# Four FNet and GEGLU layers on one core: when raw w_down, turned z and the next statistics are fetched, and how w_down pieces lie in memory

## The chip, the cores and the metric

The kernel runs on one core of one Trainium2 chip. The metric is the time of one execution in microseconds of the device (us), as the median of the runs shown. The profile is of one more execution, whose own time stands beside its span below. Names of engines: TensorE is PE (its weight loads are PEld), VectorE is DVE, ScalarE is ACT, GpSimd is POOL, SyncE is SP. SP computes nothing here: it issues loads. POOL issues nearly all stores and some loads.

## What is computed

x is 2048 tokens of 512 numbers in float32. Two kinds of layer take turns, four layers in all:

```python
def mix(x):                                   # layers 0 and 2
    z = layernorm(x)
    a, b = z @ dft_hid_re.T, z @ dft_hid_im.T          # 512 x 512 each
    return x + dft_seq_re @ a - dft_seq_im @ b         # 2048 x 2048 each
def geglu(x):                                 # layers 1 and 3
    z = layernorm(x)
    return x + (gelu(z @ w_gate) * (z @ w_up)) @ w_down   # 512 x 1792, 1792 x 512
x = geglu(mix(geglu(mix(x))))
```

Both geglu layers use the same weights.

## The kernel before, in words

**Products.** Each float32 operand is split into a high part and a low part (`split`, L148: ACT writes the high part at L150, DVE the low part at L152), and `mm3` (L205) makes one product of three matmuls (L207 to L209), each 128x128 weights against 128x512. Two-by-two blocks are multiplied with seven products for eight. The seven left operands of a block have names: A11, A12, S1, S2, S3, S4 and A22; the S are sums and differences of the four corners. They are made once, kept in DRAM as "pieces" and loaded again: `wblocks` (wb in the profile) for w_gate and w_up, `wdd` (wc in the profile) for w_down. `pieces` pairs the names: (A11, A12), (S2, S3), (S1, A22), (S4). A piece is 256 KB: 128 partitions with 256 numbers of the high part and 256 of the low part.

**geglu(w, layer)** works on one half of the tokens (w = 0 or 1), in two parts of 512.
- *Up*: the loop over n = 0 .. 13 (`up`). Even n is w_gate, odd n is w_up, for two blocks of 128 of the 1792 columns. Each n has seven products of 6 matmuls (`product`, `first`, `second`). From n = 1 on, one product of w_down of 6 matmuls is put beside it (`beside`). `finished` takes the gelu at even n (ACT, L1014) and multiplies at odd n (DVE, L1028).
- *Late*: what is left of w_down, the list `down_order(layer, w)[1]`, 36 products of 6 matmuls where all seven pairs are done this way (`SEVEN` is 7; it is 5 in the last geglu). `prepared` splits their right operands, `ended` adds and turns the results, `rows_done` stores them.

**What sets the order.** Each engine takes its instructions in a fixed order, which follows the order of the program closely; a wait of one holds those behind it on the same engine. Work that is not part of the product at hand is kept in lists:
- `queue`: `step()` is called once at each product of up and after each late product, and runs one entry; `None` is an empty turn.
- `slow`: each PACE-th (9th) step also runs one entry of `slow`. For w = 0 it holds the eight layer norms of w = 1 (`block_steps`, `norm`). For w = 1 of layer 1 it holds `terms_ahead`: for eight blocks of 128 rows of layer 2 a load of x (L235, from SP), four ACT instructions (L565 to L570) and two on POOL, which give mean and variance.
- `down_making`: for each of the seven pairs k of w_down the entries "load" (`weight_steps`, `load`: three DMAs from SP, L956 to L958, 512 KB from wdc), "sums" (four DVE instructions, L190 and L183) and four times "divide" (split a piece pair and store it from POOL, L312 and L977). They are taken four at a time at six places of layer 0 (`down_pieces`, `DOWN_RUNS`), which is pairs 0 to 3, and then two at a time at the top of each `up(n)` with n above 2 in layer 1, w = 0: pairs 4 to 6.
- The stream of pieces (`items`, `load_next` at L328, `take`): a piece of w_down may be requested from SP when it is at most `NEAR` products ahead of the one taken: 2 in up, 6 in late.

**Turned z.** `norm` turns z in blocks of 32 on DVE and stores it from POOL (L676, tile `t`). `fetch(c)` (L687) reads it back with eight DMAs of 64 KB, 128 rows of 512 B each; for w = 1 they are issued on SP, 32 in all. `first`, `second`, `fourth` and `divide` of `block_steps` make the right operands of w = 1 of it (B11, B21, T1 .. T4, B22). In w = 0 of layers 1 and 3, at n = 13, what is left in `slow` is run, and the four fetches go to the front of the queue (`ahead_of_all`), so they are run at the products of n = 13. The queue of late then begins with four empty turns, followed by the 18 entries that use the fetched blocks. After late product 12, eight loads of w_gate/w_up pieces (`ahead`, L1004) are woven into it.

**How a w_down piece lies.** `kept` stores the high parts of two names as one row of 2 KB per partition, and the low parts as the next 2 KB. `down_piece` then reads one name as two runs of 1 KB: its half of the high row and its half of the low row. S4 is alone and is one row of 2 KB.

Of the kernel before, what the change touches and what calls it, by code (L numbers as in the profile page):

```python
# [17 lines left out]
ND = D // P  # L18
# [15 lines left out]
PACE = 9  # L34
# [5 lines left out]
LEAD = 3  # L40
NK = NS // 2
SEED_AT = 3
DOWN_RUNS = ((0,0,0,0),(4,4,4,0),(4,4,4,0),2)


@with_exitstack
def fnet_geglu(ctx: ExitStack, tc: tile.TileContext, x_in, ws, wh, wgu, wdn, wdc, out):
# [32 lines left out]
    nc = tc.nc  # L80
# [56 lines left out]
    def f32(ap):  # L137
        return ap.bitcast(F32)
# [72 lines left out]
    half = slice(0, 256), slice(256, 512)  # L211
# [21 lines left out]
    def x_load(layer, i, engine=nc.sync):  # L233
        t = sb.get()
        engine.dma_start(t, rows(layer, i))  # L235
        return t
# [26 lines left out]
    def x_seeded(b, rows):  # L263

        banks = []
        for i in rows:
            t = xrows.pop((b, i))
            banks.append(ps8.get())
            seed(banks[-1], t)
            sb.put(t)  # L270
        return banks
# [24 lines left out]
    wdd = {k: dram.tile([P, 7 * 512], F32, name=f"wc{k}") for k in range(NF // 2)}  # L296
    pieces = (("A11", "A12"), ("S2", "S3"), ("S1", "A22"), ("S4",))

    def down_piece(k, name):

        i = next(i for i, names in enumerate(pieces) if name in names)
        if i == 3:
            return wdd[k][:, 3 * 1024:]
        h = half[pieces[i].index(name)]
        return wdd[k][:, i * 1024:(i + 1) * 1024].rearrange("p (h c) -> p h c", h=2)[:, :, h]

    def halves(t):
        return t[:, :512], t[:, 512:]

    def kept(place, parts):  # L310
        for t, a in zip(parts, halves(place)):
            nc.gpsimd.dma_start(a, f32(t))  # L312
# [6 lines left out]
    def load_next():  # L319
        n = stream["loaded"]  # L320
        dtype, addresses, _, _ = items[n]
        raws[n] = []
        for a in addresses:
            t = sb.get(dtype)
            to = t if dtype == F32 else f32(t)
            if len(a.shape) == 3:
                to = to.rearrange("p (h c) -> p h c", h=2)
            stream["last"] = nc.sync.dma_start(to, a)  # L328
            raws[n].append(t)
        stream["loaded"] += 1  # L330
# [101 lines left out]
    def plan(layer):  # L432

        fore, steps = FORE[layer], []
        steps += [(b, "A11") for b in range(fore)] + [(b, "A12") for b in range(fore)]
        for b in range(NB):
            if b >= fore:
                steps += [(b, "A11"), (b, "A12")]
            products = [(b, "S2"), (b, EARLY_HID), (b, "S4"), (b, MID_HID), (b, LATE_HID)]
            steps += products  # L440
        return steps
# [6 lines left out]
    NP = NF // 2  # L448
# [62 lines left out]
                items.extend((F32, (wdn[f],), plain, None) for f in range(2 * SEVEN[layer + 1, w], NF))  # L511


    queue, slow, steps_done, down_making = [], [], [0], []

    def step():
        if queue:
            run = queue.pop(0)
            if run is not None:
                run()  # L520
        steps_done[0] += 1
        if slow and steps_done[0] % PACE == 0:
            slow.pop(0)()


# [47 lines left out]
    def terms_ahead(layer, i, n):  # L573

        if i == 0:
            fresh["terms"] = x_load(layer, 0)
        x, junk = fresh.pop("terms"), sb.get()
        if i + 1 < n:
            fresh["terms"] = x_load(layer, i + 1)
        known[layer, i] = norm_terms(layer, i, x, junk)  # L580
        sb.put(x, junk)
# [156 lines left out]
    def mix(layer):  # L738
# [44 lines left out]
        def down_pieces(b, at):  # L783
            for _ in range(DOWN_RUNS[at][b]):
                if layer == 0 and down_making:
                    down_making.pop(0)()

        def six(ps, name, k, start, stop, done=None):
            w = take()
            for c in range(2):  # L790
                mm3(ps[c], z_chunk(name, k, c), w, start, stop)
            sb.put(*w)
            if done:
                sb.put(*(zparts.pop((done, k)) if done[0] == "T" else [zparts.pop((done, k))]))
            step()
# [8 lines left out]
        def a11(b):  # L804
            chain = [ps8.get() for _ in range(2)]
            for k in range(NK):
# [6 lines left out]
                else:  # L813
                    six(chain, "B11", k, k == 0, k == NK - 1, "11" if b == NB - 1 else None)
                if b == FORE[layer] - 1 and k == SEED_AT:
                    a12_seeded(0)
# [5 lines left out]
        def a12_seeded(b):  # L822

            side_banks[b] = [ps8.get() for _ in range(2)]
            for c in range(2):
                seed(side_banks[b][c], sums[b][c])
                if b:
                    put_away((layer, b, c), sums[b][c])
# [8 lines left out]
        def a12(b):  # L837
# [5 lines left out]
            for k in range(NK):  # L843
                six(side, "B21", k, False, k == NK - 1, "21" if b == NB - 1 else None)
                if k == SEED_AT:
                    if b + 1 < FORE[layer]:
# [13 lines left out]
        def s2(b):  # L860
# [12 lines left out]
            for i, k in skewed(3):  # L873
# [4 lines left out]
                else:  # L878
                    six(three, "T3", k, k == 0, k == NK - 1)
                if i == 0 and k == SEED_AT:  # L880
                    hid_banks[b] = x_seeded(b, range(2))
# [39 lines left out]
        for n, (b, what) in enumerate(plan(layer)):  # L921
            if n == len(plan(layer)) - 1:
                if layer:
                    weight_load(0)
                    weight_load(1)
                while queue:
                    step()
            in_order[0] = layer or (b, what) not in plan(layer)[:2 * FORE[layer]]
            if layer == 0 and (b, what) == (0, "S2"):
                for k in range(NP):  # L930
                    load, making = down_weight_steps(k)
                    down_making.extend([load] + making)
            if what in stages:
                stages[what](b)
            else:
                hid_groups(b, what)
# [5 lines left out]
    wblocks = {n: dram.tile([P, 7 * 512], F32, name=f"wb{n}") for n in range(NF)}  # L942
# [3 lines left out]
    def weight_steps(n, raw=wgu, place=wblocks):  # L946

        src, v = [], {}

        def load():  # L950
            src.extend(sb.get() for _ in range(4))
            for i, names in enumerate((*pieces[:3], ("S4", "A21"))):
                for name, h in zip(names, half):
                    v[name] = src[i][:, h]
            with tc.issue_after(stream["last"].ins):
                nc.sync.dma_start(src[0], raw[n, :, :512])  # L956
                nc.sync.dma_start(v["A22"], raw[n, :, 512:768])
                nc.sync.dma_start(v["A21"], raw[n, :, 768:])  # L958

        def sums():  # L960
            before, in_order[0] = in_order[0], True
            plus(v["S1"], v["A21"], v["A22"])
            minus(v["S2"], v["S1"], v["A11"])
            minus(v["S3"], v["A11"], v["A21"])
            minus(v["S4"], v["A12"], v["S2"])
            in_order[0] = before

        def divide(i):
            def run():
                before, in_order[0] = in_order[0], True  # L970
                to = place[n][:, i * 1024:min((i + 1) * 1024, 7 * 512)]
                if i < 3:
                    t = split_slot(src[i])
                    kept(to, t)
                else:
                    t = (split_side(v["S4"]),)
                    nc.gpsimd.dma_start(to, f32(t[0]))  # L977
                if place is wblocks:
                    piece_here(n, i, t)
                else:  # L980
                    sb.put(*t)
                sb.put(src[i])
                in_order[0] = before
            return run

        return load, [sums] + [divide(i) for i in range(len(pieces))]

    def down_weight_steps(k):
        return weight_steps(k, wdc, wdd)
# [17 lines left out]
    def weight_load(n):  # L1007
        for i in range(len(pieces)):
            piece_load(n, i)
# [7 lines left out]
    def geglu(w, layer):  # L1017

        gs, h, acc = {}, {}, {0: [], 1: []}
# [31 lines left out]
        making = {}  # L1051
# [35 lines left out]
        def up(n):  # L1087
# [4 lines left out]
            if n > 2:  # L1092
                for _ in range(DOWN_RUNS[3]):
                    if down_making:
# [220 lines left out]
        before_mix = w == 1 and layer < 3  # L1315
        plain_down = (layer, w) not in SEVEN
        if before_mix:
            slow.extend((lambda k=k: terms_ahead(layer + 1, k, NK)) for k in range(NK))
        if w == 0:
            norms, others = block_steps(layer, 1)  # L1320
            slow.extend(norms)
            ahead_of_all = others[:ND]
        if not plain_down and layer == 1 or layer == 3:
            sb.reclaim("x")
        first(0)
# [14 lines left out]
        elif pairs == NP:  # L1340
            load_turned(0)
        if w == 0:
            queue.extend(([None] * 4 if ahead_of_all else []) + others[len(ahead_of_all):])
        elif before_mix:
            queue.extend((lambda k=k: first_rows(layer + 1, k)) for k in range(NK))
        ahead = [(lambda n=n, i=i: piece_load(n, i)) for n in range(2) for i in range(len(pieces))]
# [154 lines left out]
```

## Time and profile before

| | us |
|---|---|
| median of 3 runs | 1626.48 |
| the runs | 1619.25, 1629.77, 1626.48 |
| the profiled execution: its own time | 1617.86 |
| its span (first to last instruction) | 1615.7 |
| layer 0 (mix) ends, layer 1 begins on PE, about | 404 |
| granted TensorE clock, mean | 0.998 |

| DMA | |
|---|---|
| moved in the span | 419.14 MB, 259 GB/s mean |
| packets under 2 KB | 106592 of 258840 |
| issued from SP (q1) | 336.16 MB |
| issued from POOL (q0) | 81.55 MB |

How to read it: the page gives the busy time of each engine as a share of the span, and for groups of instructions (line, engine, operation, tiles) their busy time, the mean of one in ns, and the idle time just before them with what ended it. The view of waits names, for an engine, who it waited for: total us, number of waits, longest. The view of stretches gives length, busy time and count of instructions, the granted clock (1.00 is full), the DMA engines' mean busy share (it can exceed 1 a little, since packets overlap) and GB/s. The timeline lists instructions with start, duration and, in brackets, the idle time before it. An "SPq" row is the issue of a DMA, not its transfer.

### The profile page before, as it was taken

The page shows a single profiled execution, that of the slowest core. Times are in us where ns is not written, and L with a number is a line of the kernel's source. Part 1 is how long each engine was busy: PE and PEld are TensorE (multiplying, and loading weights), DVE is VectorE, ACT ScalarE, POOL GpSimd, SP SyncE. Part 2 cuts the span into 40 slices and gives each one's busy share as a digit, 9 for nine tenths or more (in the row PEclk, how much of TensorE's full clock was granted, in tenths as well). Part 3 has the DMA queues.
Part 4 walks back from the last instruction along what each step waited for, and adds up shares of the span by engine and source line. Part 5 has one row for each costly group of instructions (what it writes and reads, how often), then busy time and mean ns, then how long its engine had stood idle before and what let it go on. Part 6 is the DMA issues. An engine that isn't in the chain of part 4 may idle for free. (4 is left out here: it accounts for less than half of the span.)

```text
span 1615.7 us, 22644 instructions
## 1 busy us (share of the span) xinstructions
PE 1598.9 (99%) x7008; PEld 1317.2 (82%) x7008; DVE 1133.3 (70%) x1958; ACT 885.4 (55%) x1711; POOL 260.9 (16%) x469
## 2 busy tenths in 40 slices
PE   9999999999999999999999999999999999999998
PEld 7888888888788878788788888888888888888887
DVE  8997778797689784445879967777764457743574
ACT  8955466664667552645648545565555455433460
POOL 4112121242456101100031000101400000000001
PEclk9999999999999999999999999999999999999999
DMA  9878887996988899954986866878989676895445
GB/s 359 292 266 305 284 312 263 339 327 214 335 307 320 271 309 304 248 168 138 319 285 201 269 238 224 283 246 283 267 282 301 191 222 189 309 302 175 125 150 156
DMA packets 258840, 419.14 MB, mean 259 GB/s; under 512 B 28512, under 2 KB 106592, under 8 KB 257696
## 3 DMA queue, kind: packets, MB, share of 16 engines
q1 hardware_dynamic: 234480, 336.16, 65.2%
q0 software_dynamic: 24240, 81.55, 14.2%
q8 instruction: 55, 0.90, 0.2%
q14 instruction: 65, 0.53, 0.1%
HBM read 341.31 MB, written 76.28 MB: 258 GB/s over the span
## 5 line engine op out<-in xcount | busy, mean ns | idle before, releaser
L208 PE MATMUL p<-s,s 128*128 128x512 f32 x2320 | 902.6, 390 | 0.0
L209 PE MATMUL p<-s,s 128*128 128x512 f32 x2320 | 895.8, 390 | 0.0
L207 PE MATMUL p<-s,s 128*128 128x512 f32 x2320 | 870.9, 391 | 10.7 <-DMA s<-wc 4.2
L150 ACT ACTIVATE s<-s 128x512 fp32r<-128x512 f32 (+1 forms) x809 | 454.9, 607 | 264.0 <-DVE s L183 72.9
L152 DVE TENSOR_TENSOR s<-s,s 128x512 fp32r<-128x512 f32 (+1 forms) x809 | 510.8, 669 | 121.0 <-ACT s L150 102.4
L207 PEld LDWEIGHTS p<-s,s 128*128 128x128 f32 x2320 | 436.2, 188 | 104.8 <-DMA s<-wc 5.5
L208 PEld LDWEIGHTS p<-s,s 128*128 128x128 f32 x2320 | 436.6, 188 | 91.0 <-DVE s L152 0.7
L209 PEld LDWEIGHTS p<-s,s 128*128 128x128 f32 x2320 | 436.5, 188 | 90.4
L187 DVE TENSOR_TENSOR s<-s,p 128x512 f32<-128x512 f32 x188 | 127.5, 685 | 175.6 <-PE p L209 146.5
L183 DVE TENSOR_TENSOR s<-s,s 128x512 f32<-128x512 f32 (+1 forms) x374 | 224.8, 619 | 7.9 <-PE p L208 3.7
L194 ACT ACTIVATE s<-p 128x512 f32<-128x512 f32 x232 | 134.0, 594 | 112.0 <-PE p L209 107.6
L1014 ACT ACTIVATE s<-s 128x512 f32<-128x512 f32 x84 | 52.7, 629 | 69.1 <-DVE s L187 66.9
L568 POOL TENSOR_SCALAR rstd<-rstd 128x1 f32<-128x1 f32 x40 | 22.3, 556 | 347.4 <-ACT s L567 331.9
L152 DVE TENSOR_TENSOR s<-xwide,s 128x512 fp32r<-128x512 f32 x71 | 48.3, 687 | 33.9 <-ACT s L150 33.6
L1028 DVE TENSOR_TENSOR s<-s,p 128x512 f32<-128x512 f32 x56 | 38.4, 686 | 31.5 <-PE p L209 28.2
L312 POOL DMA_DIRECT2D wb<-s x84 | 45.8, 548 | 90.1 <-ACT s L150 61.5
L190 DVE TENSOR_TENSOR s<-s,s 128x512 f32<-128x512 f32 (+1 forms) x68 | 41.1, 613 | 16.5 <-DMA s<-wdc 9.8
L150 ACT ACTIVATE s<-xwide 128x512 fp32r<-128x512 f32 x71 | 43.1, 621 | 17.2 <-DVE xwide L183 6.6
L591 ACT ACTIVATE s<-s,shift,rstd 128x512 f32<-128x512 f32 x56 | 45.0, 811 | 11.3 <-DMA s<-x 5.7
L201 ACT ACTIVATE p<-p 128x512 f32<-128x512 f32 x56 | 32.7, 585 | 27.9 <-PE p L209 27.7
L1014 ACT ACTIVATE s<-p 128x512 f32<-128x512 f32 x28 | 16.7, 598 | 52.8 <-PE p L209 49.1
L565 ACT ACTIVATE s<-s 128x512 f32<-128x512 f32 x33 | 20.7, 627 | 42.1 <-DMA s<-x 22.2
(100 smaller groups left out, 601.5 us busy)
## 6 DMA issues: line engine op xcount, KB each, us to landing
s<-ws SPq DMA_DIRECT2D x384, 256.0 KB, 4.9
s<-wb SPq DMA_DIRECT2D x294, 256.0 KB, 4.9
s<-wc SPq DMA_DIRECT2D x182, 256.0 KB, 4.7
s<-wh SPq DMA_DIRECT2D x116, 256.0 KB, 5.1
wb<-s POOLq DMA_DIRECT2D x98, 256.0 KB, 4.7
s<-x SPq DMA_DIRECT2D x59, 256.0 KB, 5.2
xwide<-ws SPq DMA_DIRECT2D x50, 256.0 KB, 4.8
wc<-s POOLq DMA_DIRECT2D x49, 256.0 KB, 6.0
```

The lines of the kernel that those rows point to most:

```text
L150: newest["ACT"] = nc.scalar.activation(hi, src, AF.Copy)
L152: newest["DVE"] = nc.vector.tensor_tensor(lo, src, f32(hi), op=ALU.subtract)
L183: nc.vector.tensor_tensor(out, a, b, op=ALU.subtract)
L187: bank_read["DVE"] = nc.vector.tensor_tensor(out, a, b, op=ALU.add)
L190: nc.vector.tensor_tensor(out, a, b, op=ALU.add)
L194: bank_read["ACT"] = nc.scalar.activation(v, src, AF.Copy)
L207: nc.tensor.matmul(ps, ah, bh, start=start, stop=False, skip_group_check=True)
L208: nc.tensor.matmul(ps, ah, bl, start=False, stop=False, skip_group_check=True)
L209: nc.tensor.matmul(ps, al, bh, start=False, stop=stop, skip_group_check=True)
L312: nc.gpsimd.dma_start(a, f32(t))
L591: nc.scalar.activation(z, x, AF.Identity, bias=shift, scale=rstd)
L1014: nc.scalar.activation(t, g, AF.Gelu_apprx_tanh)
```

## The change

Four edits go together.

1. In `mix`, the list `down_making` is built with the load of a pair moved: pairs 0 to 3 keep "load k, sums k, four divides"; at pair 4 it is "load 4, load 5, sums 4, four divides", at pair 5 "load 6, sums 5, four divides", at pair 6 "sums 6, four divides".
2. `slow` of layer 1, w = 1 begins with four empty entries, and is served each 7th step there (`pace`); w = 0 sets the pace back to 9.
3. `ahead_of_all` is filled in layer 3 alone. In layer 1 the queue of late becomes four empty turns, the four fetches, four empty turns, and the 18 entries.
4. `weight_steps` stores a w_down piece of the first three piece pairs so that each name is one row of 2 KB per partition, the 256 high numbers and then the 256 low ones: each store from POOL writes two runs of 1 KB per partition. `down_piece` reads one run of 2 KB. Pieces of w_gate and w_up stay as they were.

```diff
+MIXED = 4
...
-        h = half[pieces[i].index(name)]
-        return wdd[k][:, i * 1024:(i + 1) * 1024].rearrange("p (h c) -> p h c", h=2)[:, :, h]
+        at = i * 1024 + pieces[i].index(name) * 512
+        return wdd[k][:, at:at + 512]
...
-            if len(a.shape) == 3:
-                to = to.rearrange("p (h c) -> p h c", h=2)
...
-    queue, slow, steps_done, down_making = [], [], [0], []
+    queue, slow, steps_done, pace, down_making = [], [], [0], [PACE], []
...
-        if slow and steps_done[0] % PACE == 0:
+        if slow and steps_done[0] % pace[0] == 0:
             slow.pop(0)()
...
+                runs = [down_weight_steps(k) for k in range(NP)]
                 for k in range(NP):
-                    load, making = down_weight_steps(k)
-                    down_making.extend([load] + making)
+                    loads = [runs[k][0]] * (k <= MIXED) + [load for load, _ in runs[k + 1:k + 2] if k >= MIXED]
+                    down_making.extend([*loads, *runs[k][1]])
...
-                    kept(to, t)
+                    if place is wblocks:
+                        kept(to, t)
+                    else:
+                        for a, h in zip(t, range(2)):
+                            at = to.rearrange("p (n h c) -> p h n c", n=2, h=2)[:, h]
+                            nc.gpsimd.dma_start(at, f32(a).rearrange("p (n c) -> p n c", n=2))
...
         if before_mix:
-            slow.extend((lambda k=k: terms_ahead(layer + 1, k, NK)) for k in range(NK))
+            slow.extend([lambda: None] * 4 + [(lambda k=k: terms_ahead(layer + 1, k, NK)) for k in range(NK)])
+            pace[0] = 7
         if w == 0:
+            pace[0] = PACE
             norms, others = block_steps(layer, 1)
             slow.extend(norms)
-            ahead_of_all = others[:ND]
+            ahead_of_all = others[:ND] if layer in (3,) else []
...
         if w == 0:
-            queue.extend(([None] * 4 if ahead_of_all else []) + others[len(ahead_of_all):])
+            queue.extend([None] * 4 + others[len(ahead_of_all):ND] + ([] if ahead_of_all else [None] * 4) + others[ND:])
```

## The prediction

> **What bounds the kernel now.** I read the page's busy times first, then who TensorE (PE) waited for, then PE's matmuls counted in stretches of time, then the timelines around each loss.
>
> ```profile
> span 1615.7 us, 22644 instructions
> PE 1598.9 (99%) x7008; PEld 1317.2 (82%) x7008; DVE 1133.3 (70%) x1958; ACT 885.4 (55%) x1711; POOL 260.9 (16%) x469
> ```
> ```profile
> PE p L207 <- DMA s<-wc: 4.2, 3, 2.1
> PE p L207 <- DVE s L1028: 3.6, 1, 3.6
> PE p L207 <- ACT s L150: 2.2, 1, 2.2
> ```
> ```profile
> 436.00:446.00 10.00, 6.42 (x21) 0.83 0.84 318
> ...
> 566.00:576.00 10.00, 7.79 (x33) 1.00 1.06 371
> ...
> 645.00:655.00 10.00, 7.58 (x26) 0.83 1.14 250
> ...
> 775.00:782.00 7.00, 5.49 (x24) 1.00 1.06 377
> 781.00:1371.00 590.00, 590.00 (x2604) 1.00 0.79 251
> 1370.00:1375.00 5.00, 4.38 (x20) 1.00 1.07 377
> ```
> ```profile
> L207 PE MATMUL p<-s,s 128*128 128x512 f32 x2320 | 870.9, 391 | 10.7 <-DMA s<-wc 4.2 <-DVE s L1028 3.6 <-ACT s L150 2.2
> ```
> PE is busy for 99% of the span, and the change leaves the matmuls as they are: only PE's idle time and slowed clock can be won. The stretches (length, PE busy and count, granted clock, DMA share, GB/s) price that. A matmul lasts 0.391 us and counts wherever it is under way, so a stretch counts some 1.7 too many. The undisturbed stretch, 781 to 1371, then holds 2602.3 in 590 us: one each 0.2267 us. A stretch of length T with a count of n has lost T less (n - 1.7) x 0.2267: 436 to 446 lost **B = 5.6**, 566 to 576 **C = 2.9**, 645 to 655 **D = 4.5**, 775 to 782 **E = 1.9**, 1370 to 1375 **F = 0.9** us. Together 15.8: the most that the change can win against the profiled execution.
>
> **Part 1, raw w_down a pair ahead (B).**
> ```profile
> 429.98 0.33 SPq L957 DMA_DIRECT2D s<-wdc  x1
> ...
> 439.53 0.43 DVE L190 TENSOR_TENSOR s<-s,s 128x256 f32<-128x256 f32 x1 [6.79 <-DMA s<-wdc]
> ...
> 440.87 0.68 DVE L1028 TENSOR_TENSOR s<-s,p 128x512 f32<-128x512 f32 x1
> ...
> 441.61 0.80 PE L207 MATMUL p<-s,s 128*128 128x512 f32 x1 [3.58 <-DVE s L1028]
> ```
> ```profile
> 441.60:445.10 3.50, 3.49 (x8) 0.51 0.67 229
> ```
> In layer 1, w = 0, the loop takes two entries of the list of w_down work at each n above 2. At n = 3 they are "load pair 4" and "sums of pair 4", so the sums stand on VectorE's (DVE's) queue while the load is on its way. DVE sits 6.79 us, the multiplication for the next block (L1028) behind it comes late, and PE idles 3.58 us. Then the granted clock is 0.51 for 3.5 us: 8 matmuls where 15.4 fit, 1.7 us more. With the change n = 3 takes "load 4, load 5", n = 4 takes "sums 4, first split". One n is 48 matmuls (42, and 6 of a product of w_down), 10.9 us, and the load landed 9.5 us after its issue, so the sums find it there. Pair 5 is loaded at n = 3 and used at n = 7, pair 6 loaded at n = 6 and used at n = 9. I take B as gone: **-5.6**; it can't win more, and 0 if something else is as late. Behind it L187 and L152 wait for PE and ACT as they do everywhere. What it costs: pair 5's three DMAs (512 KB) now fall just ahead of 436, where DMA moves 318 GB/s: at that rate they are 1.6 us of all DMA engines, on SyncE's (SP's) queue ahead of raw w_gate/w_up and x loads that are used a whole n later; this cover hides it, and without it the price is 1.6 us. Its four slots stay held for three n longer: 0 by the same cover.
>
> The Trainium skill, page "TensorE: Matmul & The Clock Gate", section "What's actually happening", has the clock halve after an idle window of about 3.4 us. By that the 2.18 us wait of D (below) would cost no clock, and D would be 2.2 and the whole gain 2.3 us smaller. The trace disagrees: the row 645 to 655 has a granted clock of 0.83 after a wait of 2.2 us, so I count D in full.
>
> **Part 2, statistics begin later (D).**
> ```profile
> 631.41 0.41 SPq L235 DMA_DIRECT2D s<-x  x1
> ...
> 637.25 2.58 SPq L235 DMA_DIRECT2D s<-x  x4
> ```
> ```profile
> 643.50 0.63 ACT L565 ACTIVATE s<-s 128x512 f32<-128x512 f32 x1 [6.16 <-DMA s<-x]
> ...
> 649.12 0.61 ACT L150 ACTIVATE s<-s 128x512 fp32r<-128x512 f32 x1
> ```
> ```profile
> 640.00:680.00 40.00, 37.58 (x159) 0.96 1.06 293
> 680.00:720.00 40.00, 40.00 (x178) 1.00 0.50 158
> 720.00:760.00 40.00, 40.00 (x178) 1.00 0.41 132
> ```
> In layer 1, w = 1, ScalarE (ACT) waits 6.16 us for a row of x, and then works off the statistics of several row blocks in a row; the split (L150) that PE needs stands behind them and starts at 649.12. PE had waited 2.18 us for it, and the clock fell as at B. The loads are in flight where the DMA share is 1.06. The change puts four empty entries ahead and takes one each 7 steps for each 9: the first statistics stand at step 35 for step 9, the last at 84 for 72. A step is 10.9 / 7 = 1.56 us, so the first moves 40 us back, to about 667, and nearly all of them into stretches of share 0.41 to 0.50, where a load should land in time. All 8 still end ahead of the last of the 100 steps, so the next layer's first rows find them. Nothing is added: the same 4 ACT and 2 POOL instructions and one load each. **-4.5**; with the cover gone (a late row there too) 0, no loss beyond since the same queue order would then only move.
>
> **Part 3, turned z fetched beside late products (C).**
> ```profile
> 536.08 8.63 SPq L687 DMA_DIRECT2D s<-t  x8
> ...
> 547.70 10.18 SPq L687 DMA_DIRECT2D s<-t  x20
> 557.98 10.02 SPq L328 DMA_DIRECT2D s<-wc  x15
> ```
> ```profile
> 545.00:555.00 10.00, 10.00 (x46) 8.30 (x45) 5.46 (x9) 5.03 (x10) 0.00 (x0) 1.00 0.61 174
> ...
> 570.00:575.00 5.00, 2.79 (x12) 2.00 (x12) 5.00 (x10) 3.78 (x9) 0.00 (x0) 1.00 1.06 375
> ```
> ```profile
> L687 SPq DMA_DIRECT2D s<-t x64: 303/430/1230, 536.1 to 1355.3; - x64
> ```
> ```profile
> s<-wc SPq DMA_DIRECT2D x182, 256.0 KB, 4.7
> ```
> Layer 1, w = 0: 20 fetches of 64 KB in a row hold SP for 10.18 us at a DMA share of only 0.61, and no w_down piece (wc) is issued meanwhile; then 15 pieces come at once, the share goes to 1.06, and PE waits at 570. The change leaves layer 3 as it is and in layer 1 moves all 32 fetches to the steps after late products 4 to 7, eight at each. The pieces of products up to 10 now stand ahead of them. Were SP not ahead of PE, the block would hurt: seven products cover 7 x 6 x 0.2267 = 9.5 us, 8 fetches are 8 x 0.43 = 3.4 us (plus 0.4 for a piece), and the piece of product 14 would be issued at 15.2 us, land (median 4.7) at 19.9, and be wanted at 13.6: 6.3 us of waiting. But SP was ahead: it issued the first fetch, which stands at the top of n = 13, at 536, and PE gets there 630 matmuls (12 + 42 + 12 x 48) and B after 404, near 553. With 17 us in hand nothing is late; with half, nothing is; with none, 6.3 and 1.7 for the clock against today's 2.9. I take **-1.4**, half of C, since the row has the lead but a block of this length was never seen behind late products; ends -2.9 and +5.1. DVE gains an emptier stretch (it is busy 5.00 of 5.00 us at 570) and takes the z splits later, the last four after products 34 and 35, six products (8 us) ahead of the first use of T4; cost 0 with that cover, two splits of 0.7 us without.
>
> **Part 4, rows of 2 KB (E, F).**
> ```profile
> DMA packets 2558, 3.32 MB, mean 369 GB/s; under 512 B 203, under 2 KB 1693, under 8 KB 2556
> ```
> ```profile
> DMA packets 4184, 7.75 MB, mean 387 GB/s; under 512 B 464, under 2 KB 464, under 8 KB 4181
> ```
> ```profile
> L687 POOL DMA_DIRECT2D s<-t x52 | 28.4, 549 | 17.0 <-DMA s<-t 5.1 <-DMA xwide<-t 4.8 <-DVE s L183 3.6
> ...
> L312 POOL DMA_DIRECT2D wc<-s x42 | 22.7, 543 | 77.0 <-ACT s L150 68.3 <-DVE s L152 7.7 <-issue 0.7
> ...
> L1266 POOL DMA_DIRECT2D x<-wide x8 | 5.3, 663 | 185.3 <-DVE wide L190 185.3
> ```
> 156 of the 182 piece loads (26 pairs x 6 pieces) read 128 rows of 2 KB for 256 of 1 KB. The first of the rows on packets is 577 to 586, saturated and mostly 1 KB; the second is 20 to 40, saturated and nearly all 2 KB: 369 against 387 GB/s, 5%. The 15 pieces above are 3.9 MB: 10.7 us at the one rate, 10.2 at the other. So the late piece comes 0.5 us earlier: E **-0.5**, F **-0.5**; ends 0 and all of it for both. In return 42 stores on POOL write 256 runs of 1 KB each. The nearest POOL rows are 128 runs (0.549 us) and 512 runs (0.663): between 0.01 and 0.12 us more each, 0.3 to 5 us over 400 us of a POOL busy 16%. What reads them again is SP, and it has already waited for such a store:
> ```profile
> SPq L328 <- DMA wc<-s: 3.7, 2, 3.0
> ```
> A store that lands up to 0.1 us later (two packets for one) lengthens these two waits by as much, on a queue 17 us ahead: 0, and 0.2 without that lead.
>
> The Trainium skill, page "DMA: Bandwidth & Descriptors", section "Where 436 GB/s comes from", says of transfers between HBM and SBUF that the limit of HBM, about 358 GB/s, binds. By that longer rows bring nothing in a saturated stretch, E and F stay, and the sum is 1.0 us smaller. Both rows lie above 358, so the trace speaks against that limit here.
>
> **The sum.** -5.6 - 4.5 - 1.4 - 0.5 - 0.5 = -12.5. The profiled execution took 1617.86 us (2.2 outside its span): 1605.4. The median of the three runs, 1626.48, is 8.6 above that execution, and the runs differ by 10.5. The work on PE is the same in all, so I take the difference for longer waits of the kinds above, most of which the change removes: I leave a third, 2.9 us (ends 0 and 8.6). Forecast **1608.3 us**. All at its best gives 1617.86 - 15.8 = 1602.1; the sum with the whole 8.6 gives 1614.0.
>
> **The rivals.**
> 1. The wait only moves: B or D is replaced by another late load, say pair 5's 512 KB delaying a raw w_gate/w_up load at n = 3, or the last statistics meeting the first rows of x near 760. For it speaks that each shift of the list moves the whole order on SP; against it the shares of 0.41 to 0.50. Price one stall like B or D, 4.5 us: 1612.8.
> 2. Other side: the block of 32 fetches starves the late products. If each takes 1.08 us, as the first eight did (8.63 us), and SP has no lead, the piece of product 14 is issued 32 x 1.08 + 1.6 = 36.2 us after product 4 begins, lands at 40.9 and was wanted at 13.6: 27.3 us of waiting and 1.7 for the clock, in place of C. Time 1608.3 + 1.4 + 29.0 = 1638.7. From 15.1 us of waiting on (1626.48 - 1609.7 - 1.7) the change ends slower than before. The lead of 17 us speaks against it.
> 3. The rows of 2 KB do nothing (reads as slow as before) and C stays: 1608.3 + 1.0 + 1.4 = 1610.7.
>
> **How the numbers follow.** About 1% (16 us) is what can be told from no change here: faster is below 1610.2, slower above 1642.7. The forecast's case, both big waits gone and nothing of their size in place, has 0.68 and lies between 1602 and 1615; somewhat over half of it is under 1610.2: 0.39 faster, 0.29 same. Rival 1 has 0.15 (0.02 of it under 1610.2), rival 3 0.11 (0.03 under), rival 2 0.06, half of it past 1642.7 (its worst with the whole 8.6 is 1644.4). Faster 0.44, same 0.53, slower 0.03. Range 1601 to 1620: it takes in the first and third rival and the bound of 1602.1, and leaves out rival 2 and the worst of rival 1.
>
> **What would show it.** B right: no DVE wait on wdc above 1 us between 404 and 604, granted clock 1.00 from 436 to 446. D right: no ACT wait on x near 640, clock 1.00 there. C right: wc pieces issued on SP between 536 and 558, and fetches after them; wrong: PE waiting for wc in these late products for more than the 2.1 us of now. E and F right: waits at the late products of layer 1 w = 1 and layer 3 w = 0 shorter, and packets under 2 KB down by 30,000 to 40,000 (156 x 256 fewer from the reads, up to 42 x 256 more from the stores). The forecast is wrong if PE's waits sum to more than 4 us after, or if the median stays above 1620 with those waits gone.

## The result, and the profile after

The median of five runs after the change is 1611.43 us (1610.99 to 1613.62). Five runs of the kernel before, taken in turn with them, have a median of 1626.48 (1619.25 to 1629.77). The ratio is 0.9927 with an interval of 0.9905 to 0.9949 (it is not the quotient of the two medians, which is 0.9907): faster by 0.7%, and the interval ends short of 1. By the prediction's own bound of 1% (faster is below 1610.2) this still counts as the same. The profiled execution took 1611.43 us, the forecast was 1608.3, its range 1601 to 1620. The runs also lie closer together: 2.6 us from end to end, against 10.5 before. One run of the kernel before, of 2000.72 us at a granted clock of 0.753, timed beside e11_no_stats and e12_no_pair, is left out below.

The page after:

```profile
span 1609.7 us, 22615 instructions
...
PE 1597.4 (99%) x7008; PEld 1316.5 (82%) x7008; DVE 1132.5 (70%) x1958; ACT 885.1 (55%) x1711; POOL 271.7 (17%) x469
...
DMA packets 238872, 419.14 MB, mean 260 GB/s; under 512 B 28512, under 2 KB 66656, under 8 KB 237728
```

PE's work is unchanged, and there are 39,936 fewer packets under 2 KB (106592 less 66656), exactly the 156 x 256 of the reads. The stores, for which the prediction allowed up to 42 x 256 more, added none: POOL's queue has 24240 packets before and after. Who PE waited for after (total us, number, longest), and PE's stretches at the places where it lost time before, with one more, 1216 to 1232 (length, PE busy and count, granted clock, DMA share, GB/s):

```profile
PE p L208 <- ACT s L1019: 4.4, 1, 4.4
...
PE p L208 <- DMA s<-wc: 1.1, 1, 1.1
```
```profile
436.00:446.00 10.00, 10.00 (x46) 1.00 1.01 381
566.00:576.00 10.00, 10.00 (x46) 1.00 1.03 368
645.00:655.00 10.00, 10.00 (x46) 1.00 1.11 268
763.00:770.00 7.00, 5.88 (x26) 1.00 1.05 388
1216.00:1232.00 16.00, 11.56 (x41) 0.79 0.95 287
1370.00:1375.00 5.00, 5.00 (x23) 1.00 1.05 388
```

A full stretch of 10 us counts 46. So B, C, D and F are gone, E is left with 7 - (26 - 1.7) x 0.2267 = 1.5 us, and in layer 3 near 1220, where the kernel before lost nothing, there is a new loss, **G** = 16 - (41 - 1.7) x 0.2267 = 7.1 us. It gives back more than half of the 13.5 us won at B, C, D and F (5.4 + 2.8 + 4.4 + 0.9 by the sum below). PE's wait there is 4.4 us; the rest is half clock. (Line numbers shift by one to five with the change: L208 to L210 are the three matmuls, L1019 the gelu, L564 a row's sum, L327 the wc load, L686 the fetch.)

The losses of a whole kernel are summed over its matmuls from 20 us on: the time from one start to the next above 0.2267 us, where it is 0.05 us or more. They are used below for every run. An execution's time less this sum changes little: 1617.86 - 15.9 = 1602.0 before, 1611.43 - 9.2 = 1602.2 after, and between 1601.4 and 1603.7 in all fourteen traces. So the sum tells, within some 2 us, where the time went.

What stands at G, in the timeline after (SyncE, ScalarE and TensorE; in brackets the idle time before):

```profile
1213.14 4.10 SPq L245 DMA_DIRECT2D s<-x  x4
...
1216.02 0.29 ACT L569 ACTIVATE shift<-mean,rstd 128x1 f32<-128x1 f32 x1 [0.24 <-POOL rstd L568]
1222.79 0.63 ACT L564 ACTIVATE s<-s 128x512 f32<-128x512 f32 x1 [6.47 <-DMA s<-x]
...
1224.69 0.58 ACT L1019 ACTIVATE s<-p 128x512 f32<-128x512 f32 x1
...
1225.32 0.80 PE L208 MATMUL p<-s,s 128*128 128x512 f32 x1 [4.44 <-ACT s L1019]
```

A row of x is issued in four pieces from 1213.14 to 1217.24. ACT wants it at 1216.3, before the last piece is even issued, and stands for 6.47 us with the gelu for PE's next block behind it. This is D's pattern in another layer.

### The profile page after: what moved, and what is told of

The parts are those of the page before. It is cut to its first block, busy times and chain, and to the rows that moved or that the text cites. A ratio compares the mean times of both kernels' runs of the same rounds, so it can differ in the third digit from the quotient of the medians.

```text
span 1609.7 us, 22615 instructions
## 1 busy us (share of the span) xinstructions
PE 1597.4 (99%) x7008; PEld 1316.5 (82%) x7008; DVE 1132.5 (70%) x1958; ACT 885.1 (55%) x1711; POOL 271.7 (17%) x469
## 2 busy tenths in 40 slices
DMA packets 238872, 419.14 MB, mean 260 GB/s; under 512 B 28512, under 2 KB 66656, under 8 KB 237728
## 3 DMA queue, kind: packets, MB, share of 16 engines
q0 software_dynamic: 24240, 81.55, 14.3%
## 4 chain that ended last, share of the span: by engine, by line
PE 94%; DMA 3%; DVE 1%; ACT 1%; issue 0%; SPq 0%; POOL 0%; DVEq 0%; ACTq 0%; POOLq 0%
PE p L208 31%; PE p L209 31%; PE p L210 31%; DMA s<-x 1%; DMA xwide<-x 1%; DMA s<-wc 1%; PE p L809 1%; DMA begun<-wide 0%; DVE s L153 0%; DMA s<-wb 0%; DVE s L184 0%; DMA s<-begun 0%; DVE s L188 0%; ACT s L151 0%; SPq L1271 0%
## 5 line engine op out<-in xcount | busy, mean ns | idle before, releaser
L210 PE MATMUL p<-s,s 128*128 128x512 f32 x2320 | 893.7, 389 | 0.0
L208 PE MATMUL p<-s,s 128*128 128x512 f32 x2320 | 867.2, 390 | 5.9 <-ACT s L1019 4.4
L208 PEld LDWEIGHTS p<-s,s 128*128 128x128 f32 x2320 | 436.0, 188 | 98.7 <-ACT s L1019 4.9
L210 PEld LDWEIGHTS p<-s,s 128*128 128x128 f32 x2320 | 436.2, 188 | 90.7
L1019 ACT ACTIVATE s<-s 128x512 f32<-128x512 f32 x84 | 52.8, 629 | 60.2 <-DVE s L188 50.5
L1019 ACT ACTIVATE s<-p 128x512 f32<-128x512 f32 x28 | 16.7, 597 | 63.3 <-PE p L210 59.8
L564 ACT ACTIVATE s<-s 128x512 f32<-128x512 f32 x33 | 20.7, 626 | 46.4 <-DMA s<-x 27.9
```

What stands on the lines that cost most here:

```text
L208: nc.tensor.matmul(ps, ah, bh, start=start, stop=False, skip_group_check=True)
L210: nc.tensor.matmul(ps, al, bh, start=False, stop=stop, skip_group_check=True)
L1019: nc.scalar.activation(t, g, AF.Gelu_apprx_tanh)
```

## The experiments

My theory before the first runs: each edit removes the loss that it was meant for, and G is edit 3's doing by way of the count of steps. `step()` serves `slow` at each 9th step of a count that runs through the whole program. Edit 3 puts eight more entries in the queue of layer 1's late products: 22 + 8 + 8 = 38 for 36 products, so two extra steps are run at its end (30 entries needed none). Counted through the program, layer 3, w = 0 begins at step 758 for 756, and its first norm still falls on 765: seven steps in, for nine, that is two steps or 3 us earlier. The rivals: G comes from the moved statistics or from the rows' new timing (then edit 3 alone would not show it); and, for the 8.6 us by which the median before stood above its profiled execution, that B alone varies from run to run.

**e1_pair, e2_stats, e3_fetch, e4_rows: each edit alone on the kernel before.** Their diffs are the hunks of the change's diff: edit 1 is `runs`/`loads`, edit 2 `pace` and the four empty entries, edit 3 `ahead_of_all` and the queue of late, edit 4 `down_piece`, `load_next`'s rearrangement and the stores. The kernel before had a median of 1623.21 beside them (26 runs).

> The kernel before with edit 1 alone: raw w_down loaded a pair ahead (pairs 4 to 6). Theory (each edit takes away its own wait): the wait of DVE for wdc near 433 to 440 (6.8 us) and the PE idle behind it (B, 5.6 us with the slow clock) are gone, the losses C (2.9), D (4.5), E (1.9) and F (0.9) stay about as they were, and no loss appears near 1220: profiled time near 1612, median some 6 us under that of before, ratio 0.994 to 0.998. Rival (any edit reshuffles the order and the waits just move): B may go, but other losses of the same size come up, and the sum of the losses stays at 16 us or more: ratio 0.998 to 1.003.

Measured: 1614.77 us, ratio 0.9947 (0.9926 to 0.9967).

```profile
436.00:446.00 10.00, 10.00 (x46) 1.00 1.00 358
563.00:573.00 10.00, 6.65 (x22) 0.83 1.07 371
```

B is gone, whole. The late products lose 5.4 us at 563 for 2.8 in this execution, at a DMA share of 1.07. That edit 1 moved a part of its gain there is not shown: C is 2.7 and 5.8 us in two more executions of the kernel before (e9_before_a and e10_before_b).

> The kernel before with edit 2 alone: next layer's statistics begin later (layer 1, w = 1). Theory: the ACT wait for x near 637 to 643 and loss D (4.5 us with the slow clock) are gone, B, C, E and F stay, no loss near 1220: ratio 0.995 to 0.998. Rival (the late statistics meet the late products): D goes but E at 775 grows by 2 us or more, or a wait comes up between 655 and 775: ratio 0.998 to 1.002.

Measured: 1622.02 us, ratio 0.9982 (0.9960 to 1.0003): no gain that can be told.

```profile
436.00:446.00 10.00, 6.07 (x20) 0.76 0.84 313
...
645.00:655.00 10.00, 8.85 (x38) 1.00 1.14 199
```

D falls from 4.4 to 1.7 us and keeps its clock, but the profiled execution lost more than before at 438 (6.8), 571 (5.3) and 780 (4.0). The loss at 780 has grown as the rival expected; but it is between 1.2 and 3.7 us in the executions of the kernel before alone, so this trace does not settle it.

> The kernel before with edit 3 alone: fetches of turned z in layer 1 put beside the late products. Theory: loss C near 570 (2.9 us) goes or halves, B, D, E and F stay. The longer queue is emptied with two extra steps at the end of the late products, so the count of steps is two higher from there on and the layer norms of layer 3, w = 0 come two steps (3 us) earlier against the products: the wait of ACT for x and a PE loss of 4 to 7 us near 1220 to 1230, which the changed kernel has, come up here as well. Time then 1 to 4 us over before: ratio 1.000 to 1.004. Rival (that wait in layer 3 comes from another edit or from chance): no loss near 1220, time 2 to 3 us under before: ratio 0.997 to 0.999.

Measured: 1624.42 us, ratio 0.9996 (0.9976 to 1.0015).

```profile
563.00:573.00 10.00, 10.00 (x46) 1.00 0.78 205
...
1232.00:1248.00 16.00, 11.91 (x41) 0.79 1.06 284
```
```profile
1239.54 0.63 ACT L565 ACTIVATE s<-s 128x512 f32<-128x512 f32 x1 [6.13 <-DMA s<-x]
```

C is gone and G is there, 7.1 us, with neither the statistics nor the rows changed: the rival for G falls. The edit wins one loss and buys a bigger one. (This execution took 1628.40 us, the longest of the ten, and lost 9.3 us at B.)

> The kernel before with edit 4 alone: w_down pieces in rows of 2 KB. Theory: packets under 2 KB fall by 40,000, the late pieces come about 0.5 us earlier, so C, E and F each shrink by 0.5 us, B and D stay: 1 to 2 us, ratio 0.998 to 1.000. Rival A (the waits at late products hang on the rate at which pieces land and on more than the 5% seen): C, E and F go altogether, 5 us: ratio 0.995 to 0.998. Rival B (rows make no difference): C, E and F as before, ratio 1.000.

Measured: 1614.47 us, ratio 0.9948 (0.9929 to 0.9967), far more than the 1.0 us of the prediction. The profiled execution took 1609.37 us, the shortest of the eight by 3.4. In it C and F are gone and E is 0.6 us, nearly as rival A has it, but B is 2.8 us and D 3.0 as well, neither with a slowed clock. Its losses sum to 7.3 us; by the 1602 us that remain in each trace, the median run must lose some 12 (an estimate).

```profile
L977 POOL DMA_DIRECT2D wc<-s x42 | 30.4, 726 | 53.1 <-ACT s L150 40.1 <-ACT s L176 7.8 <-DVE s L152 4.5
```

A store with two runs of 1 KB takes POOL 0.726 us for 0.543: 0.18 us more, above the bound of 0.12, 7.7 us in all. None of PE's waits names such a store.

**e6_reads and e7_writes: edit 4 in halves.** The first has the reads of 2 KB and the old stores, the second the new stores and the old reads.

```diff
+        at = i * 1024 + pieces[i].index(name) * 512
+        return wdd[k][:, at:at + 512]
...
+                        for a, h in zip(t, range(2)):
+                            at = to.rearrange("p (n h c) -> p h n c", n=2, h=2)[:, h]
+                            nc.gpsimd.dma_start(at, f32(a).rearrange("p (n c) -> p n c", n=2))
```

> The kernel before with the reads of w_down pieces alone made rows of 2 KB; the stores stay as they were, so the products of w_down take half of another piece's numbers and the output is not the reference's. Every engine's order of instructions is that of the kernel before. Theory rate (edit 4 gained because the pieces land sooner): E and F go or halve and C goes, 4 to 9 us, ratio 0.994 to 0.997. Theory order (edit 4 gained because its stores, taken as dearer when the order was written, changed the order of the products between 115 and 620 us): only E and F shrink, 1 to 2 us, ratio 0.998 to 1.000.

> The kernel before with the stores of w_down pieces alone made two runs of 1 KB; the reads stay two runs of 1 KB, of places that now hold other numbers, so the output is not the reference's. Every engine's order is that of edit 4 alone. Theory order: B, C and D as small as with edit 4 alone, 5 to 8 us, ratio 0.995 to 0.997. Theory rate: the losses of before stay, ratio 0.999 to 1.001, or a little over through the longer stores (0.18 us each on POOL).

Measured, beside 1622.32 for the kernel before (21 runs): e6_reads 1618.90, ratio 0.9975 (0.9954 to 0.9997); e7_writes 1620.67, ratio 0.9977 (0.9954 to 0.9999). By ratio that is 4.1 and 3.7 us, about edit 4's 8.4 together; by the medians it is 3.4 and 1.7, and the interval of each half nearly reaches 1. PE's longest wait, at B, with the reads alone and with the stores alone:

```profile
PE p L207 <- DVE s L1026: 3.7, 1, 3.7
```
```profile
PE p L207 <- DVE s L1033: 4.3, 1, 4.3
```

The losses at B, C, D and E are 5.5, 1.8, 4.5, 0.6 with the reads alone and 6.1, 1.8, 2.4, 1.8 with the stores alone, against 5.4, 2.8, 4.4, 1.9 before. So with the reads alone E falls to a third and C by a third: this lies between the two theories, as the ratio does. As to the order: with e6_reads every engine has its instructions in the order of before, while with e7_writes all five have e4_rows' order. By line and tiles this differs from before in 323 of PE's 7008 places, in 42 of the 1447 DMA issues on SP and in 14 of POOL's 469 instructions (two executions of the kernel before differ in 9, 0 and 0). So the form of the stores changes the order, which is settled when the program is built; that it does so because the new stores are counted as dearer is my reading, not shown. But the theory of order expected B, C and D as small as with edit 4 alone, and with that same order B is 6.1 here for 2.8 there, and C is not gone; only D is small. What the order is worth, and why B was 2.8 in e4_rows, stays open.

**e5_shift: the whole change, with the two steps taken back in layer 3.**

```diff
             pace[0] = PACE
+            steps_done[0] -= 2 * (layer == 3)
```

> The changed kernel with the count of steps set back by two at the start of layer 3, w = 0, so that the eight layer norms there stand at the same products as before the change. Theory (the two extra steps of edit 3 moved the norms ahead, so that ACT waits for a row of x that is still on its way): the PE loss of 7.1 us near 1220 to 1231 goes, nothing else changes: 1604 to 1606 us, ratio to before 0.988 to 0.990. Rival (the loads of x in layer 3 are late through the traffic around them, wherever the norms stand by two steps): a wait of 3 to 5 us stays within 1200 to 1260, 1609 to 1612, ratio 0.992 to 0.993.

Measured: 1604.43 us (1603.49 to 1605.36), ratio 0.9893 (0.9862 to 0.9923).

```profile
763.00:770.00 7.00, 5.53 (x25) 1.00 1.05 388
1216.00:1232.00 16.00, 16.00 (x72) 1.00 0.98 245
```
```profile
1213.73 3.85 SPq L245 DMA_DIRECT2D s<-x  x4
...
1220.79 0.63 ACT L564 ACTIVATE s<-s 128x512 f32<-128x512 f32 x1 [1.90 <-PE p L210]
```

G is gone. The row of x is issued at nearly the same time as after the change (1213.73 for 1213.14), but ACT comes to it 4.5 us later (1220.79 for 1216.3), behind the gelu instead of ahead of it, and does not wait for it. That shows the cause of G. The kernel's losses sum to 3.0 us, and it is the best of all that ran. The intervals of its ratio and of the change's overlap, and they were not timed side by side; what tells them apart is that the runs' times do not overlap and that the trace shows 7.1 us at one place in the one and none in the other.

**e8_no_fetch: the whole change without edit 3.** The two `ahead_of_all` lines and the queue of late as before.

> The changed kernel without edit 3 (the fetches of turned z back at n = 13 of layer 1, the queue and the count of steps as before). Theory (edit 3 brings the wait of layer 3 by its two extra steps, and the wait at the late products that it takes away is taken away by the rows of 2 KB as well): no loss near 1220, none above 1 us near 570: 1603 to 1606, ratio 0.987 to 0.990. Rival (edit 3 is what took C away): a wait for wc of 1 to 3 us near 560 to 575, 1606 to 1609, ratio 0.990 to 0.992.

Measured: 1607.64 us, ratio 0.9919 (0.9894 to 0.9944); no loss at 1220, and 1.8 us from 565 on, near where C was. It is not C's wait: PE waits there 1.0 us for DVE, and only 0.2 for a piece of w_down.

```profile
PE p L208 <- DVE s L184: 1.0, 1, 1.0
```

So with the rows of 2 KB the wait for pieces all but goes without edit 3, as the theory said, but "none above 1 us near 570" failed, and the time is in the rival's range. Edit 3 as it stands takes away 1.8 and adds 7.1; with the count mended it is worth 1607.64 - 1604.43 = 3.2 us (same chip).

**e9_before_a and e10_before_b: the kernel before, profiled twice more.**

> The kernel before once more, unchanged, for a second look at one execution. Theory (the median of before stands above the execution profiled first because the wait of DVE for wdc, B, is at the low end there): an execution of 1621 us or more has a loss B of 7 to 10 us, against 5.4 in the first, with the rest within 2 us. Rival (the difference lies in C, D and E, or outside the losses): B stays at 5 to 6 us and the difference stands elsewhere.

> The kernel before a third time, as the last one: the time over 1602 us is the sum of the losses within 1 us, and the loss B differs most between executions (theory), or another does (rival).

Measured: 1623.59 and 1624.00 us. PE's waits of the first and of the second:

```profile
PE p L207 <- DVE s L1028: 4.4, 1, 4.4
PE p L207 <- ACT s L150: 4.0, 2, 3.3
```
```profile
PE p L207 <- ACT s L150: 2.9, 2, 2.2
PE p L207 <- DVE s L1028: 2.7, 1, 2.7
```

Losses at B, C, D, E: 6.2, 2.7, 6.8, 3.7 in the first, 4.6, 5.8, 6.7, 1.2 in the second, against 5.4, 2.8, 4.4, 1.9 in the profiled execution before; the sums of all losses are 21.9, 20.3 and 15.9. So of the 5.7 and 6.1 us that these two took longer, 4.9 and 3.8 lie in the same four places, and all of them vary, by 1.6 to 3.1 us; the theory that B alone varies falls. In the second, 1624.00 - 20.3 is 1603.7, so 1.7 us of its excess is not in the losses, more than the 1 us expected.

**e11_no_stats and e12_no_pair: e5_shift without edit 2, and without edit 1.**

> The changed kernel with the count of steps set back by two in layer 3 and without edit 2 (the statistics of layer 2 as early as before). Theory: the ACT wait for x and loss D come back near 640 to 650, nothing else: 1604.4 plus 3.0 (D with rows of 2 KB) to 4.5 us (D as before): 1607.4 to 1609. Rival (D was the work of late transfers that the other edits have thinned): 1604 to 1606.

> The changed kernel with the count of steps set back by two in layer 3 and without edit 1 (raw w_down loaded right ahead of its sums). Theory: the DVE wait for wdc and loss B come back near 438, 2.8 us (as with edit 4 alone, no slow clock) to 9 us: 1607 to 1613, and the runs spread by 5 us or more for the 2 us of now. Rival (edit 1 took away more than B): 1614 or more.

Measured, beside 1624.47 for the kernel before (seven runs): 1611.36 us, ratio 0.9917 (0.9889 to 0.9945), and 1611.51, ratio 0.9929 (0.9904 to 0.9954). What cost PE most in the one and in the other (total us, number, longest):

```profile
PE p L208 <- ACT s L151: 3.1, 2, 1.8
```
```profile
PE p L208 <- DVE s L1032: 4.6, 1, 4.6
```

Without edit 2, D is back at 641 and 655 (4.2 and 1.9 us, where 3.0 to 4.5 in all was expected), and the time is 6.9 us above e5_shift, over the 1609 expected; alone on the kernel before the same edit was worth 1.2 us, with an interval that holds 0. Without edit 1, B is back whole (7.1 us), and the time is 7.1 us above. These two differences are between chips; by the ratios, each to the kernel before beside it, they are 3.9 and 5.8 us, and the intervals overlap with e5_shift's. What shows the causes is the losses, which the traces have at these places. The times of e12_no_pair do not spread more than those of e5_shift (2.1 for 1.9 us): that part of what was expected fell, as B alone does not make the spread.

## Why the prediction was right or wrong

- **B, pair loaded ahead, -5.6.** Right in mechanism and size: 10.00 busy at full clock from 436 to 446 in the kernel after and in e1_pair; DVE's waits between 404 and 604 name no wdc any more. Taken out again, B comes back at 7.1. The price of pair 5's transfers was nothing, as said.
- **D, later statistics, -4.5.** Right in size for the whole change (10.00 busy, 645 to 655), and wrong in half of the mechanism. The first statistics were to move 40 us back, to about 667, into stretches where a load lands in time. After the change the first, second and fourth of the eight stand here (the third at 652.09):

```profile
633.55 0.63 ACT L564 ACTIVATE s<-s 128x512 f32<-128x512 f32 x1 [4.00 <-DMA s<-x]
...
637.04 0.62 ACT L564 ACTIVATE s<-s 128x512 f32<-128x512 f32 x1
...
666.07 0.63 ACT L564 ACTIVATE s<-s 128x512 f32<-128x512 f32 x1 [3.66 <-DMA s<-x]
```

  and the second to the fourth before the change here:

```profile
644.37 0.62 ACT L565 ACTIVATE s<-s 128x512 f32<-128x512 f32 x1
...
646.30 0.62 ACT L565 ACTIVATE s<-s 128x512 f32<-128x512 f32 x1
646.91 0.62 ACT L565 ACTIVATE s<-s 128x512 f32<-128x512 f32 x1
```

  So the first begins ten us earlier than before (633.55 for 643.50; 8.2 of them are B and C, won ahead of it), and ACT still waits for its row, 4.00 us for 6.16. What changed is that the statistics stand apart: before, four of them follow that wait within 4 us. In e11_no_stats, where D is back, five follow a wait of 4.94 us within 8.3. That fits the part of the working that has the statistics in a row hold up the split for PE; the part that rests on the DMA share did not come about. (The working also had the first statistics of before at step 9 of that half; the count carried in from the half before puts them at step 6, and after the change at 35 as said. The step moved 45 us back and the instruction did not: on ACT the order follows the order of the program only loosely here.) Alone, edit 2 left 1.7 us of D.
- **C, fetches beside late products, -1.4 of 2.9.** The sign was right and the half was too little: C went whole, with edit 3 alone too; with the rows of 2 KB, little of the wait was left for edit 3 to take (e8_no_fetch). SP had its lead: the first fetch is issued at 537.62 for 536.08 before, the last by 563.4 for 557.9. And the block did not go out in one piece; in the timeline after, w_down pieces stand between the fetches:

```profile
537.62 1.74 SPq L686 DMA_DIRECT2D s<-t  x4
539.53 0.41 SPq L327 DMA_DIRECT2D s<-wc  x1
...
551.67 4.86 SPq L686 DMA_DIRECT2D s<-t  x9
556.70 0.34 SPq L327 DMA_DIRECT2D s<-wc  x1
557.08 3.28 SPq L686 DMA_DIRECT2D s<-t  x7
```

  Rival 2, which starved these products, is thereby excluded.
- **E and F, rows of 2 KB, -0.5 each.** E fell by 0.5, and F, all 0.9, went. But in the three executions of the kernel before E is 1.9, 3.7 and 1.2 us and F 0.9, 0.1 and 0.3, so single traces do not show that the rows did it. Edit 4 was also priced as a faster transfer alone. In its own run it won 8.4 us; by ratio about half of that comes with the reads alone and half with the stores alone, which change the order of the instructions. The prediction had no term for an edit that reorders the program; what that order is worth is not shown. In the whole change edit 4 overlaps with edits 1 to 3: the four single ratios multiply to 0.9873, and the whole is 0.9927. G is in e3_fetch's ratio too, so it is not what makes the difference; but C goes in the trace of edit 3 and in that of edit 4, and half of B goes in that of edit 4 and all of it in that of edit 1.
- **The step that failed: "The change leaves layer 3 as it is".** The lists of layer 3 are the same, but not the count by which they are served: +7.1 us, a missing term. Rival 1 had the mechanism (another late load takes the place of B or D, 4.5 us, 0.15), but looked for it in layer 1 and near 760, and its price was D's. By its own test ("wrong if PE's waits sum to more than 4 us after") the forecast's case did fail: 4.4 at G alone.
- **A third of the 8.6 us left, +2.9.** Nothing of it was left: the median after is that of the profiled execution. It was right to put the excess to waits of the same kinds (e9_before_a, e10_before_b), and wrong to leave a third when nearly all of these waits were removed.
- **The sum.** Against the profiled execution of before, -12.5 was forecast and -6.4 measured. With C larger by 1.5 and F by 0.4, the edits won 14.4 by these terms, less 7.1 for G is 7.3; small losses and the ends of the span make the rest. Against the forecast, G's 7.1 us stand on one side, and on the other the 2.9 that were not left and the 1.9 more at C and F: so 1608.3 stood only 3.1 us from 1611.4 in part by luck, since errors of opposite sign met.

## What to carry to other kernels

Where side work is served by a count of steps, an edit that adds or removes a step anywhere moves all side work behind it: count the steps at the head of every later stage before saying that a stage is untouched, and fix the phase of each stage by hand (here one subtraction, 7 us). Then look in the trace where the work came to stand: two steps moved G's reader onto a late load, while 29 steps did not move the first statistics back at all (D). ScalarE takes its instructions in the order that was fixed when the program was built, and paid here for a late load with everything behind it, so a load's due time is set by when its reader stands in line, not by when its result is wanted. Single edits on a kernel with several waits in a row do not add up: judge each also by taking it out of the whole.

## What the runs showed of the hardware

The granted clock changes on a fixed grid of 3.413 us: in the clock's records of the kernel before, full clock lasts 436.91 and 204.80 us between slow stretches, 128 and 60 times 3.413, and every slow stretch that a wait brings on lasts 3.41 or 6.83 us in all runs. Cut by this grid, with the first window ending where half clock begins, the stretches of PE are, in the kernel before:

```profile
571.30:574.71 3.41, 1.75 (x8) 1.00 1.05 381
574.71:578.12 3.41, 3.41 (x17) 1.00 1.06 381
646.39:649.80 3.41, 1.23 (x7) 1.00 1.20 195
649.80:653.21 3.41, 3.17 (x7) 0.50 1.11 262
```

and at G in the kernel after:

```profile
1220.25:1223.66 3.41, 0.64 (x3) 1.00 0.99 213
1223.66:1227.07 3.41, 1.75 (x4) 0.50 1.06 307
1227.07:1230.49 3.42, 3.42 (x9) 0.50 1.00 400
```

C's wait of 2.1 us lies across the edge of a window, 1.66 us in this one, and the next window keeps full clock; D's 2.18 us fall into one window, and the next has half clock. Over all fourteen traces, between 20 and 1590 us, a window at full clock with 1.80 us or more of PE idle was followed by half clock each time (20 windows), and of the 38 with 0.6 to 1.68 us one was (1.53 us, in e1_pair). A window at half clock with 0.6 us or more of idle was followed by another at half clock each time (8 windows, as the second row of G), and one with 0.24 or less never (21 windows). So a wait costs clock by how much of it falls into one window, about half, and where the wait falls on the grid differs from execution to execution (the first record of the clock begins 4.3 to 7.3 us after the first instruction): a wait of 2.1 us costs its length alone, or 1.7 us of half clock on top. The Trainium skill, page "TensorE: Matmul & The Clock Gate", section "What's actually happening", calls the window free-running and 3413 ns long, and these records agree with that; it lets the clock fall after an idle window, and here a window half idle was enough.
